# Forward transform over s of a spectral filter with three real products per complex one, and its edge column worked inside the last units

## The chip, the cores and the metric

The kernel runs on one core of a Trainium2 chip. The metric is the device time in microseconds (us) of one execution, and the time of a kernel is the median of several executions. A profile is one further execution, recorded by the hardware. The engines are called as in the profile: PE is TensorE (matmuls; PEld its weight loads), DVE is VectorE, ACT is ScalarE, POOL is GpSimd, SP is SyncE, which issues most DMAs.

## The reference

Two branches start from the layernorm of x, and their product is added to x:

```python
def _A_ref(x, w_r, w_i):
    B, S, D = x.shape
    X = jnp.fft.rfft2(x, axes=(-2, -1))
    X = X * (w_r + 1j * w_i)
    return jnp.fft.irfft2(X, (S, D), axes=(-2, -1))

def _B_ref(x, w1, w2):
    h = _silu(jnp.einsum("bsd,df->bsf", x, w1))
    return jnp.einsum("bsf,fd->bsd", h, w2)

x = A_x
xn = _layernorm(x, axis=-1)
s = _A_ref(xn, A_w_r, A_w_i)
g = _silu(_B_ref(xn, B_w1, B_w2))
return x + s * g
```

S is 2048, D is 1024, the hidden width is 3584, and everything is float32. The filter has 513 columns; the last, k = 512, is the edge column.

## The kernel before

**Products.** All matrix products run on fp16 halves: each factor is split into a high and a low part, and high·high, high·low and low·high are summed in PSUM. ACT makes a high part, DVE the low one. The first product (`pa`, L456) makes the hidden rows in 112 groups of 24 matmuls of 512 columns. The second (`pb`, L539 to L541) runs seven combined products m of halved operands, each in 8 groups j of 42 matmuls; a group is two *half products* of 21. Its weights come in tiles `jr`, are split by `w2_gen` into `w` and, for m = 4 and 5, are first summed by an accumulating DMA issued from POOL (`join`, L416). `acc` evacuates a group on DVE.

**Spectral filter.** `fd_gen` transforms along d, by 16 steps, and stores the halves of real and imaginary part in DRAM (`vd`). `f_gen` transforms along s in 16 *units* u (q = u//4, j = u%4). For a unit, `mat` (L947) issues 36 matmuls on the constants `kq` and the loaded `vq`: a step by 4 × 128 rows, each with a matmul of 256 columns that holds the real and imaginary part side by side (L954) and two of 128 that add the crossed terms (L955, L956). They fill one PSUM tile `fx` of 1024 columns; there are two buffers (tag `ft`). ACT copies half of the tile to `xc`, because the next additions need two inputs of which only one is read from PSUM: DVE's `xb` and `xd` (L1004, L1005), then a radix-4 step to `X`, the multiplication by the filter weights (`T`, L1019 and L1020), the sums `T` in place, `yb` and `yd` (L1036, L1037), and `Z` (L1055, most on DVE, a share on POOL). ACT's high part (L981) and DVE's low part (L986) of Z go to `zq`, a tile of four units with one buffer, which is stored to `zd` behind each fourth unit.

**Edge column.** `xsv` collects 24 values per row: the edge column of X, copied by POOL, and the filter's weights there. `edge_gen` is a job of its own behind `f_gen`: 12 small POOL copies (L1078 to L1081) into the tile `edge`, nine float32 matmuls with permutation matrices `perm` (`eps`, L1085 to L1087, a tile of tag `ft`), 31 POOL operations on 16 or fewer elements (L1095), a scaling and the halves `zp`, which a DMA turns over into `zps`.

**Inverse.** `i_gen` transforms back, along s (`iu`, L1204 and L1212) and along d (`id`, L1294). Its first job needs `zt` loaded from `zd`, and POOL's copy of `zps` into `zt` (L1173).

**What sets the order.** Each engine executes in the order in which this code issues. The outer loop issues one half product, and then `work` (L1447) issues one slot of the weight queue `wq` and up to three slots of the queue `bg` of spectral jobs. These are generators; a slot runs one to its next yield. A unit of `f_gen` has four slots, and its matmuls stand in the third. `work` ends when its own estimate of DVE's work (`clock`, filled by `meter` from `COST`) runs ahead of that of PE, so the number of slots per half product isn't fixed. `defer(n, ...)` issues something n half products later; `tile_of` and `store` do that for tiles of partial sums.

```python
COST = {"DVE": ("dve", 0.12, 1.05e-3), "PE": ("pe", 0.0, 0.4215e-3)}
...
clock["dve"] = max(clock["dve"], clock["pe"] - 1.0)
for _ in range(3):
    if clock["dve"] > clock["pe"] + LEAD or hold[0] or slot(bg) == PAUSE:
        break
```

Of the kernel before, what the change touches and what calls it, by code (L numbers as in the profile page):

```python
# [2 lines left out]

# [40 lines left out]
def make_constants():  # L44
# [16 lines left out]
    k = np.stack([-np.sin(th), np.cos(th), np.sin(th)], 3)  # L61
# [66 lines left out]
def spectral_ffn(ctx, tc, x, w_r, w_i, w1, w2, ca, kc, ci, tw, pm, out):  # L128
# [19 lines left out]
    vd = [dp.tile([128, 4, 4, 2, 256], F16, name=f"vd{j}") for j in range(4)]  # L148
    zd = [dp.tile([128, 4, 2, 1024], F16, name=f"zd{c}") for c in range(4)]
# [62 lines left out]
    COST = {"DVE": ("dve", 0.12, 1.05e-3), "PE": ("pe", 0.0, 0.4215e-3)}  # L212
# [190 lines left out]
    def w2_gen():  # L403
# [123 lines left out]
    def load_parts(m, j):  # L527
        for k in READS[m]:
            if (k, j) in part:
                continue  # L530
            t_ = tile_of(H["p"], [128, 512], F32, f"pl{m}_{j}_{k}", *home(m, j))
# [36 lines left out]
    def acc(m, j, ps, cols=slice(0, 512)):  # L568
# [7 lines left out]
        def keep(k, t_):  # L576
            store("pt", 3, lambda: nc.sync.dma_start(pd[k, j], t_))
# [217 lines left out]
    def fd_gen(c):  # L795
# [62 lines left out]
        o, sp = {}, {}  # L858

        def high_r(j):  # L860
            sp[j] = ap.tile([128, 4, 2, 256], F16, name=f"Rs{c}_{j}", tag="Rs", bufs=2)
            nc.scalar.activation(sp[j][:, :, 0], o[j], AF.Copy, scale=2.0**-21)

        def low_r(j):
            nc.vector.scalar_tensor_tensor(sp[j][:, :, 1], o[j], 2.0**-21, sp[j][:, :, 0], op0=OP.mult, op1=OP.subtract)
            defer(2, lambda: nc.sync.dma_start(vd[j][:, :, c], sp[j]))

        for j in range(4):
# [11 lines left out]
            o[j] = r.rearrange("a (q r) k -> a q (r k)", r=2)  # L880
            yield 3.9
# [36 lines left out]
    def open_f():  # L918
# [3 lines left out]
        B["k"], B["v"], B["w"], B["z"] = {}, {}, {}, {}  # L922

    def f_gen():
# [12 lines left out]

        def load_w(u):
# [8 lines left out]
        def mat(u):  # L947
            q = u // 4
            ps = pt.tile([128, 4, 2, 128], F32, name=f"fx{u}", tag="ft")
            v, k = B["v"].pop(u), B["k"][q]  # L950
            for c in range(4):
                o = ps[:, c].rearrange("m r k -> m (r k)")
                for n, (kh, vh) in enumerate(((0, 0), (0, 1), (1, 0))):
                    nc.tensor.matmul(o, k[:, c, kh, 1], v[:, c, vh], start=(n == 0), stop=False)  # L954
                    nc.tensor.matmul(ps[:, c, 0], k[:, c, kh, 2], v[:, c, vh, 128:256], start=False, stop=False)  # L955
# [669 lines left out]
```

## Time and profile before

| | us |
|---|---|
| median of 3 executions (lowest, highest) | 1237.54 (1236.69, 1238.83) |
| the profiled execution | 1235.84 |
| its span | 1234.1 |
| PE busy in it | 1220.7 |
| DVE busy | 999.0 |
| ACT busy | 467.6 |
| POOL busy | 117.3 |

The span runs from the first to the last recorded instruction; the rest of an execution's time lies around it. A row of a timeline gives the start and the duration of an instruction in us, then engine, line, operation, the tile written and the tiles read (`Z<-yb`), the shape of an operand (partitions x elements) and in brackets how long the engine had stood idle before, and what ended that. A row of a group gives busy us and mean ns of one. The parts of the kernel lie along the span as follows: first product to about 636 us, with `fd_gen` from 156 to 555; second product from there to the end; the units from 583 to 845; the inverse from 890.

### The profile page before, as it was taken

The page shows a single profiled execution, that of the slowest core. Times are in us where ns is not written, and L with a number is a line of the kernel's source. Part 1 is how long each engine was busy: PE and PEld are TensorE (multiplying, and loading weights), DVE is VectorE, ACT ScalarE, POOL GpSimd, SP SyncE. Part 2 cuts the span into 40 slices and gives each one's busy share as a digit, 9 for nine tenths or more (in the row PEclk, how much of TensorE's full clock was granted, in tenths as well). Part 3 has the DMA queues.
Part 4 walks back from the last instruction along what each step waited for, and adds up shares of the span by engine and source line. Part 5 has one row for each costly group of instructions (what it writes and reads, how often), then busy time and mean ns, then how long its engine had stood idle before and what let it go on. Part 6 is the DMA issues. An engine that isn't in the chain of part 4 may idle for free.

```text
span 1234.1 us, 19097 instructions
## 1 busy us (share of the span) xinstructions
PE 1220.7 (99%) x7033; PEld 625.2 (51%) x7033; DVE 999.0 (81%) x1970; ACT 467.6 (38%) x614; POOL 117.3 (10%) x245
## 2 busy tenths in 40 slices
PE   8999999999999999999999999999999999999998
PEld 5545445444544454445545555554455555555545
DVE  7687988899798898896969899985186678798886
ACT  4865344333554565444433222122032222243212
POOL 2330000001000000010001121114111111000000
PEclk9999999999999999999999999999999999999999
DMA  7487476655758898759898999997989999998576
GB/s 253 134 172 187 135 224 201 185 152 161 223 172 237 276 283 242 217 177 279 207 283 224 283 259 198 276 256 246 293 207 278 286 289 331 315 332 325 200 261 260
DMA packets 271102, 293.67 MB, mean 238 GB/s; under 512 B 40096, under 2 KB 198816, under 8 KB 270624
## 3 DMA queue, kind: packets, MB, share of 16 engines
q1 hardware_dynamic: 250992, 233.66, 65.7%
q10 hardware_dynamic: 15984, 51.45, 12.0%
q0 software_dynamic: 4032, 7.34, 3.5%
q8 instruction: 55, 0.90, 0.3%
q14 instruction: 39, 0.32, 0.1%
HBM read 185.95 MB, written 102.25 MB: 234 GB/s over the span
## 4 chain that ended last, share of the span: by engine, by line
PE 75%; DVE 11%; DMA 9%; issue 2%; ACT 1%; SPq 0%; POOL 0%; DVEq 0%; ACTq 0%; POOLq 0%
PE pa L456 45%; PE pb L539 8%; PE pb L541 8%; PE pb L540 8%; DVE Z L1055 2%; DMA wq<-in_A_w_i_dram 2%; DMA sd<-s 2%; PE id L1294 2%; DMA zd<-zq 1%; DMA ht<-hd_sum_d 1%; DVE T L1020 1%; DVE w L254 1%; PE iu L1204 1%; ACT xp L709 1%; PE iu L1212 1%
## 5 line engine op out<-in xcount | busy, mean ns | idle before, releaser
L456 PE MATMUL pa<-xnT,w 128*128 128x512 f16 x2688 | 585.2, 379 | 1.1 <-ACT w L251 0.7
L456 PEld LDWEIGHTS <-w 128*128 128x128 f16 x2688 | 262.2, 98 | 311.6 <-DVE w L254 1.3
L539 PE MATMUL pb<-w,ht 128*128 128x512 f16 (+2 forms) x812 | 300.4, 372 | 0.0
L540 PE MATMUL pb<-w,ht 128*128 128x512 f16 (+2 forms) x812 | 300.4, 372 | 0.0
L541 PE MATMUL pb<-w,ht 128*128 128x512 f16 (+2 forms) x812 | 300.3, 372 | 0.0
L541 PEld LDWEIGHTS <-ht 128*128 128x128 f16 x812 | 79.4, 98 | 91.0
L539 PEld LDWEIGHTS <-ht 128*128 128x128 f16 x812 | 79.5, 98 | 86.7
L540 PEld LDWEIGHTS <-ht 128*128 128x128 f16 x812 | 79.4, 98 | 86.7
L465 ACT ACTIVATE h<-pa,s 128x512 f32<-128x512 f32 x112 | 75.5, 678 | 122.9 <-PE pa L456 111.0
L251 ACT ACTIVATE w<-jr,sc 128x512 f16<-128x512 f32 x98 | 68.1, 713 | 77.8 <-PE pb L541 22.1
L254 DVE SCALAR_TENSOR_TENSOR w<-jr,sc,w 128x512 f16<-128x512 f32 x98 | 71.1, 744 | 2.1 <-ACT w L251 2.1
L254 DVE SCALAR_TENSOR_TENSOR hoone<-h,hs,hoone 128x2048 f16<-128x2048 f32 x28 | 65.6, 2344 | 7.9 <-ACT hoone L251 7.9
L251 ACT ACTIVATE hoone<-h,hs 128x2048 f16<-128x2048 f32 x28 | 56.0, 1998 | 36.5 <-DVE h L499 24.3
L251 ACT ACTIVATE hosum<-hr,hs 128x1536 f16<-128x1536 f32 x28 | 44.1, 1574 | 64.1 <-DVE hr L495 26.8
L981 ACT ACTIVATE zq<-Z,zs 128x1024 f16<-128x1024 f32 x16 | 18.4, 1149 | 103.9 <-DVE Z L1055 57.0
L494 DVE TENSOR_TENSOR hr<-h 128x1024 f32<-128x1024 f32 x28 | 34.2, 1221 | 24.4 <-ACT h L465 24.3
L254 DVE SCALAR_TENSOR_TENSOR hosum<-hr,hs,hosum 128x1536 f16<-128x1536 f32 x28 | 50.7, 1812 | 3.1 <-ACT hosum L251 3.1
L251 ACT ACTIVATE w<-w1r,rs 128x1024 f16<-128x1024 f32 x28 | 31.9, 1144 | 47.0 <-DVE w L254 31.8
L274 DVE TENSOR_REDUCE m<-w1r 128x1 f32<-128x1024 f32 x28 | 33.8, 1210 | 16.1 <-DMA w1r<-in_B_w_dram 16.1
L632 ACT ACTIVATE pl<-pl,c 128x512 f32<-128x512 f32 (+2 forms) x28 | 17.6, 657 | 70.1 <-DVE pl L608 41.6
L954 PE MATMUL fx<-vq,kq 128*128 128x256 f16 x192 | 43.2, 273 | 0.0
L955 PE MATMUL fx<-vq,kq 128*128 128x128 f16 x192 | 42.0, 219 | 0.0
(219 smaller groups left out, 1524.8 us busy)
## 6 DMA issues: line engine op xcount, KB each, us to landing
w1r<-in_B_w_dram SPq DMA_DIRECT2D x28, 512.0 KB, 6.2
hd_sum<-hosum SPq DMA_DIRECT2D x56, 256.0 KB, 2.9
hd_one<-hoone SPq DMA_DIRECT2D x56, 256.0 KB, 3.7
hd_dif<-hoone SPq DMA_DIRECT2D x56, 256.0 KB, 3.2
w2m<-in_B_w_dram SPq DMA_DIRECT2D x28, 512.0 KB, 5.2
ht<-hd_dif ACTq DMA_DIRECT2D x32, 448.0 KB, 6.3
jr<-in_B_w_dram SPq DMA_DIRECT2D x56, 256.0 KB, 6.8
ht<-hd_sum ACTq DMA_DIRECT2D x32, 448.0 KB, 6.4
```

What stands on the lines that cost most here:

```text
L251: nc.scalar.activation(hi, raw, AF.Copy, scale=scale)
L254: nc.vector.scalar_tensor_tensor(lo, raw, scale, hi, op0=OP.mult, op1=OP.subtract)
L274: nc.vector.tensor_reduce(m1[:, i:i + 1], raw[i], axis=AX.XY, op=OP.max, apply_absolute_value=True)
L456: nc.tensor.matmul(ps, w[:, wh, d], xt[:, xh, d], start=(n == 0), stop=(n == 23))
L465: nc.scalar.activation(hq[:, 2 * (c % 2) + f % 2], ps, AF.Silu, scale=s1[:, f:f + 1])
L494: tt(sums[:, 0:2], hq[:, 0::2], hq[:, 1::2], op=OP.subtract)
L539: nc.tensor.matmul(ps, hh[:, 0], w[:, 0], start=first, stop=False)
L540: nc.tensor.matmul(ps, hh[:, 0], w[:, 1], start=False, stop=False)
L541: nc.tensor.matmul(ps, hh[:, 1], w[:, 0], start=False, stop=last)
L954: nc.tensor.matmul(o, k[:, c, kh, 1], v[:, c, vh], start=(n == 0), stop=False)
L955: nc.tensor.matmul(ps[:, c, 0], k[:, c, kh, 2], v[:, c, vh, 128:256], start=False, stop=False)
L1055: eng.tensor_tensor(Z[:, ns, pos], x0[:, :, ls], x1[:, :, ls], op=o_)
```

## The change

**Three products.** With a constant c + i·s and data a + i·b, the changed `mat` makes c·(a+b), (s−c)·b and (−s−c)·a; the real and the imaginary part are the first plus the second and the first plus the third. The constants `kq` hold cos, sin − cos and −sin − cos in place of −sin, cos and sin. The sum a+b is the third operand: `fd_gen` makes it (`total`, one DVE addition a step), splits it (`both`, one ACT and one DVE instruction) and stores it (`vs`, 256 KB a step); `load_s` loads it two units ahead into `vs` tiles of its own tag with two buffers. A unit now has two PSUM tiles of 2 × 512 columns, of which 3 × 128 of each 512 are used, so it takes both buffers of `ft`. There are 36 matmuls of 128 columns.

**Sums.** ACT copies the shared product twice side by side into `xo` (two copies of 512 elements; `xo` shares tag `T1` with the products by the filter weights, `xc` is gone), DVE adds the two other products from PSUM in two additions of 512, and then `xb` and `xd` read SBUF.

**Edge column.** `edge_gen` is stepped inside units 12 to 15 instead of as a job behind them. Its tiles `edge` and `perm` come from the pool of partial sums, its PSUM tile from the pool of the products (tag `ff`), and the 16 small loads into `xsv` are issued in units 0 to 7 instead of 0 to 15.

**Room and order.** The weight tiles of the second product have 8 slots instead of 7; the eighth takes some partial sums for m = 4. The tiles `fs` and `fx` come from a pool opened after the filter's is closed. The fixed part of DVE's cost in `COST` is 0.09 until the inverse stage opens, and 0.12 from there.

```diff
-    k = np.stack([-np.sin(th), np.cos(th), np.sin(th)], 3)
+    k = np.stack([np.cos(th), np.sin(th) - np.cos(th), -np.sin(th) - np.cos(th)], 3)
...
-    COST = {"DVE": ("dve", 0.12, 1.05e-3), "PE": ("pe", 0.0, 0.4215e-3)}
+    COST = {"DVE": ("dve", 0.09, 1.05e-3), "PE": ("pe", 0.0, 0.4215e-3)}
...
-                w2t[m, q // 7] = fp.tile([128, 7, 2, 512], F16, name=f"w2_{m}_{q // 7}", tag="big", bufs=4)
+                w2t[m, q // 7] = fp.tile([128, 8, 2, 512], F16, name=f"w2_{m}_{q // 7}", tag="big", bufs=4)
...
         def high_r(j):
+            both[j] = ap.tile([128, 4, 2, 128], F16, name=f"vt{c}_{j}", tag="wd", bufs=3)
+            nc.scalar.activation(both[j][:, :, 0], total[j], AF.Copy, scale=2.0**-21)
...
+            nc.vector.scalar_tensor_tensor(both[j][:, :, 1], total[j], 2.0**-21, both[j][:, :, 0], op0=OP.mult, op1=OP.subtract)
+            defer(2, lambda: nc.sync.dma_start(vs[j][:, :, c], both[j]))
...
+            nc.vector.tensor_tensor(total[j], o[j][:, :, 0:128], o[j][:, :, 128:256], op=OP.add)
...
         def mat(u):
             q = u // 4
-            ps = pt.tile([128, 4, 2, 128], F32, name=f"fx{u}", tag="ft")
-            v, k = B["v"].pop(u), B["k"][q]
-            for c in range(4):
-                o = ps[:, c].rearrange("m r k -> m (r k)")
-                for n, (kh, vh) in enumerate(((0, 0), (0, 1), (1, 0))):
-                    nc.tensor.matmul(o, k[:, c, kh, 1], v[:, c, vh], start=(n == 0), stop=False)
-                    nc.tensor.matmul(ps[:, c, 0], k[:, c, kh, 2], v[:, c, vh, 128:256], start=False, stop=False)
-                    nc.tensor.matmul(ps[:, c, 1], k[:, c, kh, 0], v[:, c, vh, 0:128], start=False, stop=(n == 2))
-            psx[u] = ps
+            v, t_, k = B["v"].pop(u), B["s"].pop(u), B["k"][q]
+            for half in range(2):
+                ps = pt.tile([128, 2, 512], F32, name=f"fx{u}_{half}", tag="ft")
+                for i, c in enumerate((half, half + 2)):
+                    for g, src in enumerate((t_[:, c], v[:, c, :, 128:256], v[:, c, :, 0:128])):
+                        for n, (kh, vh) in enumerate(((0, 0), (0, 1), (1, 0))):
+                            nc.tensor.matmul(ps[:, i, 128 * g:128 * g + 128], k[:, c, kh, g], src[:, vh], start=(n == 0), stop=(n == 2))
+                psx[u, half] = ps
+            if u + 2 < 16:
+                defer(1, lambda: load_s(u + 2))
...
-            cps[u] = bp.tile([128, 2, 256], F32, name=f"xc{u}", tag="xc", bufs=1)
-            nc.scalar.activation(cps[u], psx[u].rearrange("m c r k -> m c (r k)")[:, 2:4], AF.Copy)
+            cps[u] = bp.tile([128, 2, 2, 2, 128], F32, name=f"xo{u}", tag="T1", bufs=1)
+            for half in range(2):
+                nc.scalar.activation(cps[u][:, half], psx[u, half][:, :, 0:128].unsqueeze(2).broadcast_to([128, 2, 2, 128]), AF.Copy)
...
+            full = cps.pop(u)
+            for half in range(2):
+                planes = psx.pop((u, half))[:, :, 128:384].rearrange("m i (r k) -> m i r k", r=2)
+                tt(full[:, half], full[:, half], planes, op=OP.add)
...
+            if u == 12:
+                B["edge"] = edge_gen()
+            if u > 13:
+                next(B["edge"])
             yield 2.8
...
+            if u == 12:
+                next(B["edge"])
+            if u > 13:
+                next(B["edge"])
             yield 2.3
...
+            if u > 13:
+                next(B["edge"])
             yield 2.5
...
+            if u > 12:
+                next(B["edge"], None)
             yield 2.9
...
-        ps = pt.tile([128, 1024], F32, name="eps", tag="ft")
+        ps = pf.tile([128, 512], F32, name="eps", tag="ff")
...
-                add(bg, edge_gen())
```

Where the instructions stand is seen in each engine's order. On PE the units' matmuls stood behind every 42 or 63 matmuls of the second product, and stand behind every 63. The edge matmuls stood 105 of them behind the last unit's; here is that place in the order before (a row is a line of the code, an operation and its tiles):

```order
L541 LDWEIGHTS ht_2_1_8059
L541 MATMUL pb_2_8256<-w_2_1_7449,ht_2_1_8059 128x512
L1085 MATMUL eps<-edge,perm 128x24
L1086 MATMUL eps<-edge,perm 128x8
L1087 MATMUL eps<-edge,perm 128x8
```

In the changed kernel they stand 21 behind the matmuls of unit 14, and 42 ahead of those of unit 15:

```order
L546 LDWEIGHTS ht_2_0_8081
L546 MATMUL pb_2_8362<-w_2_0_7167,ht_2_0_8081 128x512
L1123 MATMUL eps<-edge,perm 128x24
L1124 MATMUL eps<-edge,perm 128x8
L1125 MATMUL eps<-edge,perm 128x8
```

Counted from the last unit's matmuls they have moved from 105 behind to 42 ahead. POOL makes their input. Before, its 12 copies stood behind its share of the last unit's Z:

```order
L1055 TENSOR_TENSOR Z_8284<-yb_8248 128x2x16 x2
L1055 TENSOR_TENSOR Z_8284<-yd_8249 128x2x16 x2
L1078 COPY edge<-xsv 128x24
L1079 COPY edge<-xsv 128x8
L1080 COPY edge<-xsv 128x2
L1081 COPY edge<-xsv 128x6
```

In the changed kernel they stand behind unit 13's Z (Z_8333), and the first operations on the edge matmuls' result (L1133) ahead of unit 14's (Z_8533); from the last copies on:

```order
L1116 COPY edge<-xsv 128x24
L1117 COPY edge<-xsv 128x8
L1118 COPY edge<-xsv 128x2
L1119 COPY edge<-xsv 128x6
L1133 TENSOR_TENSOR edge<-xsv,edge 128x16 x3
L1133 TENSOR_TENSOR edge<-edge,xsv 128x16
L1133 TENSOR_TENSOR edge<-xsv,edge 128x16 x4
L1087 TENSOR_TENSOR Z_8533<-yb_8518 128x2x16 x2
L1087 TENSOR_TENSOR Z_8533<-yd_8519 128x2x16 x2
```

So the edge column's POOL work went from behind the units to between the Z of the last three. Further on POOL's queue, the first inverse job's copy of the edge column (`zt<-zps`) stood behind three of the accumulating weight DMAs that follow the edge column's work, and stands behind seven (the last six of them shown):

```order
L418 DMA jr_8704<-in_B_w_dram 128x512
L418 DMA jr_8749<-in_B_w_dram 128x512
L418 DMA jr_8785<-in_B_w_dram 128x512
L418 DMA jr_8876<-in_B_w_dram 128x512
L418 DMA jr_8908<-in_B_w_dram 128x512
L418 DMA jr_8934<-in_B_w_dram 128x512
L1213 COPY zt_8817<-zps 128x16
```

The copy has moved with the inverse stage, which begins 84 matmuls of the second product later, while the weight DMAs keep their places beside the second product.

More of the change, by code (lines that the diff above doesn't have):

```diff
@@ L2 @@
 from contextlib import ExitStack
+from types import SimpleNamespace
 import numpy as np
@@ L148, in spectral_ffn @@
     vd = [dp.tile([128, 4, 4, 2, 256], F16, name=f"vd{j}") for j in range(4)]
+    vs = [dp.tile([128, 4, 4, 2, 128], F16, name=f"vs{j}") for j in range(4)]
     zd = [dp.tile([128, 4, 2, 1024], F16, name=f"zd{c}") for c in range(4)]
@@ L576, in keep @@
         def keep(k, t_):
-            store("pt", 3, lambda: nc.sync.dma_start(pd[k, j], t_))
+            store("big" if m == 4 and j % 2 else "pt", 3, lambda: nc.sync.dma_start(pd[k, j], t_))
         def evac():
@@ L1063, in edge_gen @@
     def edge_gen():
-        bp = B["p"]
         g = nc.gpsimd
         xv = xsv
-        perm = B["perm"]
-        room, used = bp.tile([128, 1024], F32, name="edge", tag="T1", bufs=1), [0]
+        room, perm = (tile_of(H["p"], [128, 512], F32, name, "pt", 6) for name in ("edge", "perm"))
+        perm = perm[:, 0:384].rearrange("m (n k) -> m n k", n=3)
+        nc.sync.dma_start(perm, pm[:, 0:3])
+        used = [0]
+        yield
         def piece(n):
+            if used[0] + n > 512:
+                used[0] = 0
             used[0] += n
@@ L1150, in open_i @@
         C["ci"] = C["p"].tile([128, 2, 4, 2, 256], F16, name="cis")
+        COST["DVE"] = ("dve", 0.12, 1.05e-3)
         C["z"], C["k"] = {}, {}
```

36 lines of the change are left out of this document (23 added, 13 removed).

## The prediction

> **What bounds it.** I read the page's busy shares and its chain first, then the waits of PE, then the stage that the change rewrites.
>
> ```profile
> span 1234.1 us, 19097 instructions
> PE 1220.7 (99%) x7033; PEld 625.2 (51%) x7033; DVE 999.0 (81%) x1970; ACT 467.6 (38%) x614; POOL 117.3 (10%) x245
> PE 75%; DVE 11%; DMA 9%; issue 2%; ACT 1%; SPq 0%; POOL 0%; DVEq 0%; ACTq 0%; POOLq 0%
> PE tp L718 <- ACT x L709: 3.0, 3, 2.0
> PE iu L1212 <- DVE ub L1221: 1.7, 1, 1.7
> ```
>
> PE (TensorE) is busy 99% of the span. The last two rows are from the view of waits (engine and line, what it waited for; us in total, times, longest): the largest belongs to the start-up (L718 transposes x), the next is one wait in the inverse transform. So between the first matmuls and the last PE goes from one matmul to the next without a pause: the end is the sum of PE's work, and any microsecond taken from PE's instruction stream is gained, unless some engine then can't keep up and PE waits. Windows through the forward stage show who could fail (us; busy us and count of PE, weight loads, DVE, ACT, POOL; clock, DMA share, GB/s):
>
> ```profile
> 652.70:845.00 192.30, 192.15 (x1184) 103.74 (x1181) 177.60 (x328) 46.37 (x66) 32.87 (x70) 1.00 0.93 246
> 684.90:701.00 16.10, 16.10 (x100) 8.61 (x99) 10.33 (x19) 4.05 (x6) 0.47 (x2) 1.00 0.99 329
> 701.00:717.00 16.00, 16.00 (x100) 8.59 (x98) 15.90 (x32) 2.23 (x3) 3.73 (x8) 1.00 0.97 223
> 156.00:560.00 404.00, 404.00 (x2101) 193.68 (x2100) 346.83 (x681) 188.19 (x224) 19.61 (x34) 1.00 0.71 212
> ```
>
> The granted clock is 1.00. DVE (VectorE) is busy without a gap in 701–717 and idle in 684.9–701; it swings between late and stalled, while PE never notices. The slack between DVE and PE is what the change spends.
>
> **The matmuls (the gain).** One unit's matmuls and their neighbour (start us, duration us; a duration includes the pipeline, so I use differences of starts):
>
> ```profile
> 650.12 0.27 PE L954 MATMUL fx<-vq,kq 128*128 128x256 f16 x1
> 650.23 0.22 PE L955 MATMUL fx<-vq,kq 128*128 128x128 f16 x1
> 650.28 0.22 PE L956 MATMUL fx<-vq,kq 128*128 128x128 f16 x1
> ...
> 652.77 0.38 PE L539 MATMUL pb<-w,ht 128*128 128x512 f16 x1
> 895.68 2.68 PE iu L1204 x48
> 100.83 5.18 PE pa L456 x24
> L954 PEld LDWEIGHTS <-kq 128*128 128x128 f16 x192 | 18.8, 98 | 1.9
> L1204 PEld LDWEIGHTS <-zt 128*128 128x128 f16 x192 | 11.2, 98 | 1.4
> ```
>
> A unit is 36 matmuls, 12 of 256 columns and 24 of 128, in 2.65 us. After it is 36 of 128 columns, each with weights of its own. The chain of waits has the same form: 48 matmuls L1204 of 128 columns, each behind a weight load, in 2.68 us, 55.8 ns each. So 36 × 0.0558 = 2.01 us, 0.64 less, and 16 × 0.64 = **10.2 us** less. It is the same as the difference of columns: 1536 columns a unit at 5.18/24/512 = 0.42 ns. No matmul of the two products changes in number. The Trainium skill speaks against this gain ("TensorE: Matmul & The Clock Gate", § Back-to-back issue gap): it gives a stream of weight load and matmul pairs about 81 ns a matmul at 128 columns, by which, as an estimate, a unit would cost 36 × 81 = 2.92 us and the stage 4.3 us more than before. The rows of this case, 55.8 ns in such a stream, disagree.
>
> **Additions ahead of the stage.** The third operand costs 16 DVE additions, 16 low parts and 16 ACT high parts, each of 512 elements, and 16 writes of 256 KB.
>
> ```profile
> 717.54 0.68 DVE L1004 TENSOR_TENSOR xb<-fx,xc 128x512 f32<-128x512 f32 x1
> 718.14 0.68 DVE L1005 TENSOR_TENSOR xd<-fx,xc 128x512 f32<-128x512 f32 x1
> L254 DVE SCALAR_TENSOR_TENSOR w<-jr,sc,w 128x512 f16<-128x512 f32 x98 | 71.1, 744 | 2.1 <-ACT w L251 2.1
> ```
>
> By xb, 0.60 us from start to start, and a weight tile's low part of 512, 0.74, that is 16 × 1.34 = 21 us of DVE in the 156–560 window, where it has 57 us free, and DMA runs at 0.71. Cost on PE: nothing; without that cover it would be late by what is missing.
>
> **DVE inside the units.** Each unit gets two more additions of 512 elements that read PSUM, as xb does, and loses nothing: +1.20 us.
>
> ```profile
> 696.98 1.28 DVE L986 SCALAR_TENSOR_TENSOR zq<-Z,zs,zq 128x1024 f16<-128x1024 f32 x1 [5.36 <-ACT zq L981]
> 808.10 1.28 DVE L986 SCALAR_TENSOR_TENSOR zq<-Z,zs,zq 128x1024 f16<-128x1024 f32 x1 [7.98 <-ACT zq L981]
> zd<-zq SPq DMA_DIRECT2D x16, 512.0 KB, 7.2
> ```
>
> The 192.3 us window holds 13 units: 177.60/13 = 13.66 us of DVE each, 14.86 after. Units now come irregularly, after 42 or 63 matmuls of the second product; in the new order always after 63, so every 63 × 0.2158 + 2.01 = 15.6 us. DVE has 0.7 us to spare per unit, if its stalls go. These are the two in the rows: every fourth unit ACT's high part needs the one zq buffer, which the four stores to zd free (median landing 7.2 us), and DVE's low part waits for ACT. Between the stores and that high part lies less than a unit; at 15.6 us the unit gives up to 3.9 us more than the short ones of 11.7 (42 matmuls), so I count on much shorter stalls. If both stay, 13.3/13 = 1.0 us a unit is more than the spare, and DVE falls behind by some 0.3 us a unit. ACT's two copies of 512 elements a unit take the place of one; ACT is busy 46 of 192 us, so nothing. The 16 loads of 256 KB add 17 GB/s to 246, where other windows reach 329: nothing, as long as they are asked for two units ahead.
>
> Both PSUM buffers now belong to one unit, so the next unit's matmuls wait for these additions. They come 13.6 us after the unit's matmuls end. Before, the corresponding readers ended late at worst here:
>
> ```profile
> 804.24 0.22 PE L956 MATMUL fx<-vq,kq 128*128 128x128 f16 x1
> 813.63 0.68 DVE L1037 TENSOR_TENSOR yd<-T 128x512 f32<-128x512 f32 x1
> 818.05 0.68 DVE L1005 TENSOR_TENSOR xd<-fx,xc 128x512 f32<-128x512 f32 x1
> 720.35 0.22 PE L956 MATMUL fx<-vq,kq 128*128 128x128 f16 x1
> 725.59 0.68 DVE L1037 TENSOR_TENSOR yd<-T 128x512 f32<-128x512 f32 x1
> ```
>
> Unit 14's xd ended 818.73, 14.4 us behind matmuls that ended 804.30, with the 7.98 stall in it; without, 6.5. So this new wait costs between 0 and 0.8 us once; I take 0, nearer to the unit without stall.
>
> **The edge column moved inside the units.** Before, its matmuls stood 105 second-product matmuls behind the last unit's; now only 21 behind unit 14's, and their input is copied by POOL (GpSimd) behind unit 13's Z, which needs unit 13's yd. So PE gets a new wait, and behind it stand all matmuls of the kernel. The pieces, from unit 15 of before:
>
> ```profile
> 840.39 0.68 DVE L1037 TENSOR_TENSOR yd<-T 128x512 f32<-128x512 f32 x1
> 845.03 0.18 POOL L1081 COPY edge<-xsv 128x6 f32<-128x6 f32 x1
> 843.20 0.30 PE L1085 MATMUL eps<-edge,perm 128*128 128x24 f32 x2
> 845.00 0.38 PE L1085 MATMUL eps<-edge,perm 128*128 128x24 f32 x2
> 845.66 0.38 PE L539 MATMUL pb<-w,ht 128*128 128x512 f16 x1
> ```
>
> From yd's end (841.07) to the end of the last copy (845.21) are 4.14 us. On PE, the last three edge matmuls start 21 × 0.2158 + 1.80 = 6.33 us behind unit 14's, the 1.80 being the first six. With x for how long after unit 14's matmuls unit 13's yd ends, PE waits x + 4.14 − 6.33 = x − 2.2. Before, x was 814.31 − 804.30 = 10.0 there (and 726.27 − 720.41 = 5.9 for unit 7). The interval in question becomes 15.6 instead of 42 × 0.2158 + 2.65 = 11.7, which takes 3.9, and the additions give 1.2: x = 7.3 if the stall recurs. Without the stall and nothing else changed, 10.0 − 7.98 = 2.0. I take the middle, 4.6: **+2.4 us**, with 0 and 5.1 as ends.
>
> POOL's edge work now runs beside DVE's last three units:
>
> ```profile
> 590.11 0.68 DVE L1055 TENSOR_TENSOR Z<-yb 128x128 f32<-128x128 f32 x2
> 814.23 0.91 DVE L1055 TENSOR_TENSOR Z<-yb 128x128 f32<-128x128 f32 x2
> 813.85 1.03 POOL L1055 TENSOR_TENSOR Z<-yb 128x32 f32<-128x32 f32 x2 [18.74 <-DVE yb L1036]
> ```
>
> The same DVE addition takes 0.68 us alone and 0.91 beside POOL; a third more on DVE's work in the 4.14 us above is at most 1.4 us, inside the range of x. The Trainium skill says that GpSimd shares its SBUF interfaces with VectorE ("GPSIMD Engine Reference", § 1. Specifications), contending where an instruction has two SBUF inputs; these rows agree.
>
> **The inverse stage and the tail.** The first inverse unit needs POOL's small copy of the edge column, which stands behind weight joins on POOL's queue, three before and seven after:
>
> ```profile
> 890.43 0.85 POOL L1173 COPY zt<-zps 128x16 f16<-128x16 f16 x1
> L416 POOL DMA_DIRECT2D jr<-in_B_w_dram x7: 853/868/1191, 869.4 to 899.3; - x7
> DMA to landing us min/median/max: 4.4/7.8/14.9
> ```
>
> The copy ended 891.28 and L1204 started 895.68: 4.4 us of slack. The last join's load is recorded two half products, 9.1 us, ahead of the copy; at the median landing of 7.8 it costs nothing, at 14.9 it costs 14.9 − 9.1 − 4.4 = 1.4, and with three joins of 0.87 left to issue 4.0. I take **+0.5**, near the median. Larger weight tiles, a slot for partial sums in them, and the pool opened late only move storage; the last inverse matmuls end 252 second-product matmuls (54 us) before PE's end, so nothing.
>
> **Sum.** −10.2 + 2.4 + 0.5 = −7.3. The profiled execution took 1235.84 us (1234.1 and 1.7 around it), so 1228.5 by its clock; it lies 1.7 under the median of 1237.54. From the median: **1230.2 us**.
>
> **Rivals.** A: *no new wait.* DVE, evenly loaded, finishes yd within 2.2 us of the next matmuls. For it: regular intervals; against: x was 5.9 in an undisturbed unit. −10.2: 1227.3.
>
> B: *DVE becomes the bound at the end of the stage.* Stalls on zq stay, 0.3 us a unit add up over 13 units to 3.9, and x reaches 8.5 to 10. The wait at the edge matmuls is 6.3 to 7.8, with the 0.5: 1234 to 1235.6. For it: only 0.7 us spare, DMA at 0.93 of its time. Against: the stores get a longer unit to land in.
>
> C: *the joins hold the edge copy.* +4.0 in place of 0.5: 1233.7. For it: POOL waits for its loads' landing; against: the median of 7.8.
>
> D: *weight loads set the pace, and the change is slower.* If a matmul of 128 columns can't start faster than its weight load lasts, a unit is 36 × 0.098 = 3.53 us, 0.88 more: +14.1, 1251.6. It decides as soon as the spacing is over 2.65/36 = 73.6 ns. Against: L1204's loads also last 98 ns, and run at 55.8, so they overlap. The Trainium skill's 81 ns ("TensorE: Matmul & The Clock Gate", § Back-to-back issue gap) lies on this side: by it, as an estimate, +4.3 and the two waits, 1244.7.
>
> **Chances.** Forecast 0.50 (1228.4 to 1233), A 0.20, B 0.15, C 0.11, D 0.04. A measurement of this kernel tells about 0.2%, 2.5 us, from no change: faster is below 1235.1. The forecast, A, C and half of B lie there, 0.89; the rest of B is within, 0.07; D is slower, 0.04. The range 1226.5 to 1235.5 leaves out D, a little of A and the end of B.
>
> **What would show it.** Right: a unit of matmuls of 2.0 us; a wait of PE at the edge matmuls of 1 to 5 us on POOL's copies, and no wait at fx. A is shown by no such wait, B by one over 6 us or waits at fx on DVE's additions, and zq stalls in DVE's rows; C by a wait of iu on the copy of zt; D by a unit over 2.65 us. What would make it wrong altogether is a wait that I have put at nothing: the third operand's load landing late, or DVE late ahead of the stage.

## The result, and the profile after

| | before | changed |
|---|---|---|
| median of 5 executions, us (lowest, highest) | 1236.69 (1235.1, 1238.83) | 1266.55 (1264.93, 1269.16) |
| profiled execution, us | 1235.84 | 1264.93 |

The changed kernel is slower: the ratio is 1.024, interval 1.0225 to 1.0255, some 30 us, where 7 less were forecast. The page of the changed kernel has these answers to the rows shown of before:

```profile
span 1263.2 us, 19218 instructions
PE 1223.6 (97%) x7033; PEld 622.8 (49%) x7033; DVE 1039.6 (82%) x2034; ACT 482.2 (38%) x646; POOL 124.9 (10%) x245
PE 44%; DVE 27%; DMA 19%; issue 4%; SPq 3%; ACT 3%; ACTq 0%; POOL 0%; DVEq 0%; POOLq 0%
```

The chain of waits is no longer PE's: its share fell from 75% to 44%, and DVE and DMA have most of what it lost. The view of PE's waits (what it waited for; us, times, longest) says where:

```profile
PE id L1334 <- DVE sk L1348: 6.8, 1, 6.8
PE pa L458 <- ACT h L467: 6.2, 2, 3.2
PE eps L1123 <- POOL edge L1116: 5.9, 1, 5.9
PE pb L544 <- DMA ht<-hd_dif: 4.3, 2, 2.4
PE iu L1252 <- DVE ub L1261: 3.6, 2, 3.1
...
PE fa L787 <- ACT L L797: 1.5, 1, 1.5
```

Here `iu` and `id` are the inverse's matmuls along s and along d, `ub` and `sk` DVE's steps on their results, `h` the hidden rows as ACT evacuates them, and `fa` matmuls of `fd_gen`. All but 1.7 us (iu) of these waits are new. They don't account for everything, because PE's busy time rose too, although it has less to do. Windows around the wait for the edge column (busy us of PE, weight loads, DVE, ACT, POOL; then the granted clock) show why:

```profile
836.00:842.00 6.00, 6.00 (x56) 3.85 (x55) 2.23 (x4) 2.37 (x3) 0.00 (x0) 1.00 1.01 248
842.00:849.00 7.00, 1.17 (x6) 0.32 (x4) 6.96 (x12) 1.08 (x2) 2.11 (x6) 0.91 0.99 311
849.00:852.00 3.00, 2.90 (x14) 2.90 (x14) 3.00 (x8) 2.30 (x3) 2.40 (x12) 0.50 1.09 74
852.00:855.00 3.00, 3.00 (x11) 1.68 (x11) 2.90 (x7) 1.04 (x3) 1.52 (x5) 0.50 0.92 189
855.00:858.00 3.00, 3.00 (x9) 1.07 (x8) 3.00 (x4) 0.01 (x1) 3.00 (x5) 0.51 1.03 402
858.00:861.00 3.00, 3.00 (x15) 1.36 (x14) 2.35 (x4) 0.00 (x0) 0.40 (x1) 1.00 0.80 310
...
780.00:783.00 3.00, 1.12 (x7) 0.33 (x5) 3.00 (x9) 0.67 (x2) 0.89 (x3) 1.00 1.04 404
783.00:786.00 3.00, 3.00 (x16) 1.35 (x15) 2.90 (x6) 1.32 (x2) 0.00 (x0) 1.00 0.99 352
```

Behind the stop of 6 us PE's granted clock is 0.50 for 9 us, and its matmuls take twice as long (0.43 us from start to start instead of 0.22); behind the stop of 2 us at 780 it stays 1.00.

**Where the time went, by stage.** Both kernels issue the same 2688 + 2436 matmuls of the two products in the same order. I took the start of one and the same such matmul in both traces, where all work of a stage lies ahead of it in both: the 2416th of the first product (ahead of the first unit), the 881st of the second (all units and the edge column done), the last. The differences to before grow by **+12.0 us ahead of the units, +4.3 with the units and +12.8 in the inverse and the tail**, 29.1 in all. Without the gain of 10.2 the units are 14.5 worse.

### The profile page after: what moved, and what is told of

Its sections match the earlier page's. It is cut to its first block, busy times and chain, and to the rows that moved or that the text cites. A ratio compares the mean times of both kernels' runs of the same rounds, so it can differ in the third digit from the quotient of the medians.

```text
span 1263.2 us, 19218 instructions
## 1 busy us (share of the span) xinstructions
PE 1223.6 (97%) x7033; PEld 622.8 (49%) x7033; DVE 1039.6 (82%) x2034; ACT 482.2 (38%) x646; POOL 124.9 (10%) x245
## 4 chain that ended last, share of the span: by engine, by line
PE 44%; DVE 27%; DMA 19%; issue 4%; SPq 3%; ACT 3%; ACTq 0%; POOL 0%; DVEq 0%; POOLq 0%
PE pa L458 21%; PE pb L545 6%; PE pb L544 6%; PE pb L546 6%; DMA jr<-in_B_w_dram 3%; DVE w L256 2%; DMA sd<-s 2%; DVE Z L1087 2%; DMA ws<-wd 2%; DVE hoone L256 2%; DMA vs<-vt 2%; SPq L490 1%; DVE wd L377 1%; DVE hosum L256 1%; DMA ht<-hd_sum_d 1%
## 5 line engine op out<-in xcount | busy, mean ns | idle before, releaser
L256 DVE SCALAR_TENSOR_TENSOR hoone<-h,hs,hoone 128x2048 f16<-128x2048 f32 x28 | 65.7, 2345 | 11.6 <-ACT hoone L253 11.6
L995 ACT ACTIVATE xo<-fx 128x512 f32<-128x512 f32 x32 | 17.5, 594 | 73.0 <-DVE yd L1067 48.5
L276 DVE TENSOR_REDUCE m<-w1r 128x1 f32<-128x1024 f32 x28 | 33.8, 1211 | 13.2 <-DMA w1r<-in_B_w_dram 13.2
L1087 POOL TENSOR_TENSOR Z<-yb 128x32 f32<-128x32 f32 x32 | 16.1, 522 | 216.5 <-DVE yb L1066 216.5
L418 POOL DMA_DIRECT2D jr<-in_B_w_dram x28 | 24.8, 1010 | 126.0 <-DMA jr<-in_B_w_dram 47.0
```

Source lines behind the costliest of these rows:

```text
L256: nc.vector.scalar_tensor_tensor(lo, raw, scale, hi, op0=OP.mult, op1=OP.subtract)
L276: nc.vector.tensor_reduce(m1[:, i:i + 1], raw[i], axis=AX.XY, op=OP.max, apply_absolute_value=True)
L418: nc.gpsimd.dma_start(raw[n], w2_block(*todo[n], 1), accum_op=OP.add)
L995: nc.scalar.activation(cps[u][:, half], psx[u, half][:, :, 0:128].unsqueeze(2).broadcast_to([128, 2, 2, 128]), AF.Copy)
L1087: eng.tensor_tensor(Z[:, ns, pos], x0[:, :, ls], x1[:, :, ls], op=o_)
```

## The experiments

The kernel before had medians of 1236.6 to 1238.3 beside these. The last four columns are differences to before in the profiled executions, by the stages above. Each row of them is one execution: before_late and late_rows issue up to the inverse what the kernel before issues, and still have +3.2 and +1.1 in the units, most of it at the edge column's matmuls. So a term of 3 us alone says little. Kernels that leave out work (no_sum, pe_clean, b1_nosum, b1_noadds, late_rows, after_rows, pe_only) don't compute the reference; they only locate time.

| kernel | median us | ahead of units | units | inverse | sum |
|---|---|---|---|---|---|
| changed | 1266.55 | +12.0 | +4.3 | +12.8 | +29.1 |
| no_sum | 1251.47 | +1.0 | +2.2 | +14.0 | +17.2 |
| edge_later | 1266.87 | +13.9 | −7.5 | +23.6 | +30.0 |
| ht_sp | 1269.92 | +12.0 | +4.6 | +14.8 | +31.5 |
| before_late | 1255.23 | +0.2 | +3.2 | +16.6 | +20.0 |
| edge_dve | 1265.11 | +13.8 | −6.0 | +21.9 | +29.6 |
| lag0 | 1265.07 | +12.5 | +4.5 | +8.6 | +25.6 |
| fd_fix | 1263.45 | +5.9 | +7.9 | +14.1 | +27.8 |
| best1 | 1260.23 | +14.7 | −4.2 | +15.9 | +26.4 |
| pe_clean | 1242.11 | −0.1 | −10.7 | +13.8 | +2.9 |
| b1_nosum | 1251.78 | +2.4 | −3.8 | +14.8 | +13.3 |
| b1_noadds | 1254.03 | +1.7 | +7.1 | +10.3 | +19.1 |
| before_adds0 | 1244.41 | +0.0 | +3.0 | +4.0 | +7.0 |
| late_rows | 1247.46 | −0.2 | +1.1 | +10.8 | +11.6 |
| after_rows | 1262.47 | +12.4 | +2.0 | +10.5 | +24.8 |
| pe_only | 1245.01 | +0.3 | +0.1 | +8.3 | +8.8 |
| pl_pt | 1270.27 | +14.5 | +5.4 | +16.0 | +35.9 |
| fd_own2 | 1280.34 | +19.6 | +13.7 | +13.2 | +46.5 |
| best5 | 1279.85 | +18.9 | −0.3 | +24.1 | +42.8 |

### The third operand (no_sum, fd_fix, fd_own2)

```diff
-            total[j] = ap.tile([128, 4, 128], F32, name=f"vt{c}_{j}", tag="E", bufs=1)
-            nc.vector.tensor_tensor(total[j], o[j][:, :, 0:128], o[j][:, :, 128:256], op=OP.add)
...
-            nc.sync.dma_start(B["s"][u], vs[j][:, q])
+            nc.sync.dma_start(B["s"][u], vd[j][:, q, :, :, 0:128])
```

> The changed kernel without the third operand's making: fd_gen's additions, its halves and its store to vs are left out, and the units load the real part from vd in its place, as many bytes. Theory (in the stage ahead of the units ACT waits for buffers that the third operand shares with the weight sums, and for its last store, and PE then waits for ACT three times, 1.5, 3.3 and 3.1 us, with the granted clock at 0.5 behind the two long ones): these three waits go, 12 us with the clock, 1254.5. Rival (the stage is late because the units' first slots are recorded earlier, not because of these buffers): the waits stay, 1265 to 1267.

All three waits ahead of the units (fa 1.5, pa 3.2 and 3.0) are gone, 11 us with the clock, and the median is 15 lower. So the third operand's making costs it. How, is seen in ACT's timeline of the changed kernel (in brackets, how long it had stood idle and what ended that):

```profile
532.70 0.63 ACT L867 ACTIVATE vt<-vt 128x512 f16<-128x512 f32 x1 [2.82 <-DMA ws<-wd]
...
570.68 0.39 ACTq L940 DMA_DIRECT2D kq<-in_kc_dram  x1
571.12 0.69 ACT L467 ACTIVATE h<-pa,s 128x512 f32<-128x512 f32 x1 [14.95 <-DMA vs<-vt]
```

The operand's high part waits for a buffer of the ring `wd`, which it shares with the weight sums, until one of their stores lands. Later ACT's load of `kq` waits 15 us for the last store of the operand, since the units' pool takes its place. Behind both stands ACT's evacuation `h<-pa`, for which PE waits. fd_fix stores it one half product sooner and gives that load to SP:

```diff
-            defer(2, lambda: nc.sync.dma_start(vs[j][:, :, c], both[j]))
+            defer(1, lambda: nc.sync.dma_start(vs[j][:, :, c], both[j]))
...
-            nc.scalar.dma_start(t_, kf[q])
+            (nc.sync if q == 0 else nc.scalar).dma_start(t_, kf[q])
```

> The changed kernel with the store of the third operand issued one half product sooner, and the first load of kq issued by SP instead of ACT. Theory (ACT's queue stands still, first for shared buffers whose stores are late, then behind the load of kq that waits for the last store): the wait at 568 goes with its half clock, 4.5 us, and half of the one at 531, 3 us: 1258 to 1262. Rival (SP's queue, which carries the hidden rows' stores, stands still in ACT's place): no gain, 1265 to 1270.

Ahead of the units 6.1 of the 12.0 went, where 7.5 were expected, and not as expected: the wait at 568 is gone, and so is the one at fa, but the one at 531 grew from 3.2 to 4.2 us, with ACT's wait for the ring at 4.0. The units lost 3.6: PE now waits 3.2 us at fx, half of it for the operand's loads, which stand behind on SP. fd_own2 was to settle the ring:

```diff
-            both[j] = ap.tile([128, 4, 2, 128], F16, name=f"vt{c}_{j}", tag="wd", bufs=3)
+            both[j] = ap.tile([128, 4, 2, 128], F16, name=f"vt{c}_{j}", tag="vt", bufs=2)
...
-                nc.scalar.activation(junk, t_, AF.Abs, accum_out=w2m[:, i - 3:i - 2])
+                nc.scalar.activation(t_, t_, AF.Abs, accum_out=w2m[:, i - 3:i - 2])
```

> The changed kernel with the third operand's halves in a ring of two buffers of their own (the weight sums keep two, and the room is that of the scratch tile of the weights' maximum, which is now taken in place), and the first load of kq issued by SP. Theory (ACT stands still for the shared ring and behind the load of kq, and nothing else of the third operand costs time): the 12 us ahead of the units shrink to 0 to 3, 1255 to 1258. Rival (the work itself, ACT's and DVE's additions to the stage, makes PE wait): 6 us or more stay there, 1260 or more.

A miss by its own doing. The room came from taking the maximum in place, and ACT's waits show what that costs:

```profile
ACT w2m L383 <- DVE wd L376: 98.1, 17, 13.3
```

ACT may overwrite the tile only when DVE has read it, and stood still for 98 us. That the ring alone makes the first wait is therefore seen in the trace, not shown by a run. best5 is this with edge_dve and lag0. At 1279.85 it missed its forecast of 1239 to 1249 by the same cause, and says no more; no kernel here beats the one before.

> fd_own2 with the edge column later, its copy on DVE and the inverse opened two pauses sooner (first inverse matmuls at 1071), a kernel that computes all. Theory (terms add: ahead of the units 0 to 3, units -7, inverse 8 to 16): 1239 to 1249, so no gain against before. Rival (with all of its waits' causes gone it keeps most of its 10.2): 1233 or less.

### The edge column (edge_later, edge_dve)

```diff
-            if u > 13:
+            if u > 14:
                 next(B["edge"])
             yield 2.8
```

> The changed kernel with the edge column's matmuls recorded two slots later, behind unit 15's matmuls instead of 21 behind unit 14's, and the rest of the edge work as much later. Theory (PE's 6.1 us wait there is for POOL's copies behind a late unit 13, and the half clock behind it costs 3.9 more): 10 us less, 1256.5. Rival (DVE is late as a whole, and the next thing that PE needs of it waits instead, unit 15's matmuls for unit 14's additions, or the first inverse unit): 3 us less or nothing, 1263.5 to 1266.5.

The theory came true for the wait and the rival for the time. The units are 11.8 us better (from +4.3 to −7.5), some 10 of it the wait with its half clock. And the median is the same, since the inverse took 10.8 of it, and the stage ahead of the units the rest:

```profile
PE iu L1246 <- POOL zt L1215: 8.8, 1, 8.8
```

This is the joins that hold the edge copy, rival C, which the earlier stop had covered. edge_dve issues that copy on DVE:

```diff
-            nc.gpsimd.tensor_copy(zt[:, :, :, :, 0, 0], zps[:, :, c])
+            (nc.vector if c == IORDER[0] else nc.gpsimd).tensor_copy(zt[:, :, :, :, 0, 0], zps[:, :, c])
```

> The kernel edge_later with the first inverse job's copy of the edge column into zt issued on DVE instead of POOL. Theory (with the wait at the edge matmuls gone, PE reaches the first inverse matmuls sooner and there waits 8.8 us for this copy, which stands on POOL's queue behind seven weight joins): the wait goes with the half clock behind it, 12 us less than edge_later, 1255. Rival (zt or zps itself lands late, whoever copies): the wait stays, now behind DVE's copy, 1265 to 1268, or more where DVE is held by it.

Its theory held for the wait and not for the time. The first inverse matmuls now start without a wait, 34.1 us behind DVE's last low part of the units instead of 43.0 (48.3 in the kernel before), but at a later inverse unit PE waits 7.0 us for DVE's `ub`, and the inverse's term fell by 1.7 only.

### The loads of ht (ht_sp)

In the units of the changed kernel ACT waits 25.5 us for stores of zq, and 47 us for yd, the last reader of the products whose buffer `xo` now shares. The loads of ht stand behind on its queue. Below these two rows is the first of the stops, which ends with the landing of a load that ACT issued at 771.58, behind a high part for which it had waited 9.4 us:

```profile
ACT xo L995 <- DVE yd L1067: 47.2, 9, 8.4
ACT zq L1001 <- DMA zd<-zq: 25.5, 3, 9.4
...
771.56 1.15 ACT L1001 ACTIVATE zq<-Z,zs 128x1024 f16<-128x1024 f32 x1 [9.40 <-DMA zd<-zq]
782.53 0.39 PE L544 MATMUL pb<-w,ht 128*128 128x512 f16 x1 [1.88 <-DMA ht<-hd_dif]
```

```diff
-                    load_h(*seq[n + 2], k, nc.scalar)
+                    load_h(*seq[n + 2], k, nc.sync)
```

> The changed kernel with the second product's loads of ht issued from SP's queue instead of ACT's. Theory (the two waits for ht at 780 and 798 us, 2.0 and 2.6, come because the loads stand on ACT's queue behind instructions that wait for the zq store and for yd): both go, 4.6 less, 1262. Rival 1 (the loads are late by their transfer, with DMA at 1.0 of its time): no change, 1266.5. Rival 2 (SP's queue waits longer than ACT's): slower, above 1270.

Both waits went, but two others came, 5.7 us at 718 and 1.6 at 917, so the waits for ht grew from 4.3 to 7.3 us; the units' term is as before, and the median lies between the two rivals'. SP's queue is no freer. That the first stop comes from ACT's wait is read in the trace, not shown by a run; the load behind the second took 16.35 us from issue to landing, so the transfer has a part in that one. Nothing here shows how to get the loads past.

### The place of the inverse (before_late, lag0, late_rows, after_rows, pl_pt)

```diff
-                add(bg, switch(B, open_i, 6, lag=2))
+                add(bg, switch(B, open_i, 6, lag=6))
```

> The kernel before with nothing changed but four more pauses ahead of the inverse stage, so that every inverse matmul stands behind as many matmuls of the second product as in the changed kernel (the first 84 later). Theory (the inverse stage's waits in the changed kernel, 6.8 for id and 3.2 for iu, 12.8 us with the clock against before, come from this place alone, where its DVE work and loads meet those of m = 4): about 12 us slower than before, 1248 to 1250. Rival (they come from DVE's lag out of the units, the eighth slot of the weight tiles or the later pool): within 2 us of before, 1236 to 1239.

The clearest run of all: the kernel before, with only the inverse recorded 84 matmuls later, loses 16.6 us in it; the whole takes 1.0141 (1.0125 to 1.0156) times as long as before. That is more than the 12 expected. PE's and DVE's waits of before_late:

```profile
PE iu L1212 <- DVE ub L1221: 9.6, 1, 9.6
PE id L1294 <- ACT w L251: 4.1, 1, 4.1
...
DVE pl L623 <- DMA fs<-sd: 18.8, 3, 9.0
```

DVE finishes row blocks of m = 4 with filter rows `fs`, loaded from DRAM. In the kernel before it never waits for them in this stretch; here, as in the changed kernel (12.7 us), the rows have only just been made when they are due, so the load is asked for right ahead of its use, and what stands behind on DVE, the inverse's `ub`, is late for PE. late_rows reads x in their place:

```diff
-        for name, src, (tag, bufs) in (("fs", sd[c, p], tags[0]), ("fx", xs[4 * c + p], tags[1])):
+        for name, src, (tag, bufs) in (("fs", xs[4 * c + p], tags[0]), ("fx", xs[4 * c + p], tags[1])):
```

> The kernel before_late, where the last step for a row block reads x a second time in place of the filter's row from DRAM (so the filter's part of these rows is left out), with as many bytes. Theory (in before_late DVE waits 18.8 us for rows that the inverse stored just before they are reloaded, and PE for DVE): these waits go, 10 to 14 us less than before_late, 1241 to 1245. Rival (the weights' joins and DVE's load in this place make it): 1253 or more.

8 us less, not 10 to 14. The store's way goes, but DVE waits all the same:

```profile
DVE pl L623 <- DMA fs<-in_A_x_dram: 15.2, 3, 8.2
```

The load behind the longest of these waits is issued at 1050.42, 2.0 us after DVE began to wait for it, and lands at 1056.50. So it is the late asking more than the store. after_rows is the same edit in the changed kernel:

> The changed kernel, where the last step for a row block reads x a second time in place of the filter's row from DRAM (the filter's part of these rows is left out). Theory (the inverse's waits in the changed kernel are the reload's too, 12.7 us on DVE): the wait of iu goes and part of the one of id, 6 to 10 us less, 1256 to 1261. Rival (the one of id, 6.8, is the weight loads', and the gain is taken by another): 1263 or more.

It gave 1262.47: the wait of id shrank to under 1 us, and iu's grew from 3.6 to 8.9, the other way round from its theory; as its rival has it, another wait took the gain. lag0 opens the inverse two pauses sooner:

```diff
-                add(bg, switch(B, open_i, 6, lag=2))
+                add(bg, switch(B, open_i, 6, lag=0))
```

> The changed kernel with the inverse stage opened two pauses sooner, so that its first matmuls stand 42 matmuls of the second product earlier (1071 instead of 1113; 1029 in the kernel before), and its third job on at the places of before. Theory (the inverse's place is what makes DVE wait 12.7 us for rows that were stored just before, and PE for DVE): the waits at id and at the second job's iu go, 10 to 13 us less, 1254 to 1257. Rival 1 (DVE's lag out of the units makes them): they stay, 1264 to 1268. Rival 2 (zt, loaded 9 us sooner, lands late and PE waits at the first iu instead): 1258 to 1264.

The median, 1265.07, is what rival 1 forecast. In the profiled execution, the fastest of four with 1261.43, the inverse's term fell from 12.8 to 8.6 and id's wait from 6.8 to 1.1, while iu first waited 1.9 for the edge copy: by its waits in between the theory and rival 2. pl_pt puts the partial sums of m = 4 back into their pool:

```diff
-            if m == 4 and k == 0 and j % 2:
-                t_ = w2t[m, j // 2 % 2][:, 7].rearrange("p h x -> p (h x)").bitcast(F32)
```

> The changed kernel with the partial sums of m = 4 in the pool they had before instead of the weight tiles' eighth slot. Theory (the slot has no part in the inverse's waits): 1264 to 1269. Rival (weight tiles wait for partial sums stored from their slot, and id and iu behind them): 1258 or less.

1270.27: the eighth slot isn't the cause, and taking it away gains nothing.

### The gain alone, and the work it brings (best1, pe_clean, b1_nosum, b1_noadds, before_adds0, pe_only)

best1 is edge_dve, lag0 and fd_fix together with DVE's cost at 0.07. b1_nosum leaves out the third operand's making (as no_sum), b1_noadds DVE's additions in the units, and pe_clean both, with every inverse matmul at one place:

```diff
-                tt(full[:, half], full[:, half], planes, op=OP.add)
```

> All of these together (edge column later, its copy on DVE, inverse opened two pauses sooner, the third operand's store sooner, kq by SP) with DVE's fixed cost at 0.07, which puts every inverse matmul but the first job's first at the place of before. Theory (each wait has its own place and cause): what is left is the 10.2 us of gain against the two ht waits (4.6) and half of the wait at 531 (3 to 5): 1233 to 1238. Rival (the work that the change adds to DVE has to be waited for somewhere): waits of 6 us or more come up elsewhere, 1245 or more.

best1 took 1260.23, as its rival said: PE waits 5.3 and 3.0 us ahead of the units, 3.2 at fx and 6.9 at iu.

> The matmuls of the change without the work that they bring to DVE: the third operand isn't made (fd_gen's additions, halves and store are left out, the units load the real part instead) and DVE's two additions from PSUM in each unit are left out; the edge column later, its copy on DVE and the inverse opened two pauses sooner, as in best1, so that every inverse matmul stands where it stands in best1. Theory (the gain on PE is there, and DVE's added work eats it): no wait over 2 us is left, 10 us less than before, 1226 to 1231. Rival (both PSUM buffers in one unit and the matmuls' form bring waits of their own): 1237 or more.

The gain is there: −0.1 and **−10.7** up to the end of the units, with no stop of PE over 0.6 us between 50 us and 889. Then the inverse takes 13.8, and the median, 1242.11, lies in the rival's range, though not by the rival's cause. DVE's copy of the edge column stood 11.59 us for zt, and PE behind it:

```profile
893.27 0.21 DVE L1208 COPY zt<-zps 128x16 f16<-128x16 f16 x1 [11.59 <-DMA zt<-zd]
```

The last of the four loads of zt landed at 893.05, and the constants `kk` for the same matmuls at 894.13, 0.04 us ahead of PE's start: all of the first job's loads are late, not the copy alone. Here the first inverse matmuls stand 252 matmuls behind the last unit's; in the kernel before it was 336, in the changed one 294, since its last unit moved back by 126 and the inverse only by 84. So opening the inverse sooner, as in lag0, takes from the time in which zq is stored and zt loaded. No run has the new matmuls with 336.

before_adds0 gives the kernel before the additions alone:

```diff
-            tt(b.rearrange("m c r k -> m c (r k)"), pv[:, 0:2], cpy, op=OP.add)
+            for _ in range(3):
+                tt(b.rearrange("m c r k -> m c (r k)"), pv[:, 0:2], cpy, op=OP.add)
```

> The kernel before, with its own matmuls, where DVE makes xb three times over, that is two more additions of 512 from PSUM in each unit; DVE's fixed cost at 0.09 up to the inverse and the inverse opened two pauses sooner, so that every inverse matmul stands where it stands in best1. Theory (DVE has no room for 19 us more in this stretch): PE waits for DVE at fx or iu, 6 to 12 us and its half clock: 1244 to 1252. Rival (DVE has room; only the changed kernel's buffers make it late): 1236 to 1240.

The median lies at the low end of the theory's range, but by luck: PE waits only 1.3 us for DVE, at iu, not 6 to 12, so my theory that DVE has no room fell here. Two more additions a unit cost PE 0.8 us up to the last unit. The rest of the 7.0 comes at the edge column (+2.2, no more than before_late shows there without any addition) and in the inverse (+4.0), where PE waits 2.8 us for POOL's edge copy.

> best1 without the third operand's making (left out in fd_gen, the units load the real part instead), with DVE's additions in the units. Theory (the waits ahead of 640 us are those of the third operand's making, some 11 us and their half clock): 14 to 17 us less than best1, 1243 to 1246. Rival (removing one wait only lets another grow): 1252 or more.

> best1 with the third operand made, without DVE's two additions in each unit (left out), DVE's fixed cost at 0.09. Theory (the waits behind 700 us, at fx 3.2 and at iu 6.9, 1.9 and 1.3, come from DVE being late by these additions): 12 to 16 us less than best1, 1244 to 1248. Rival (they come from the place of the edge column and the inverse): within 5 us of best1, 1255 or more.

They gave 1251.78 and 1254.03, both slower than their theories and close to their rivals: against pe_clean the additions cost 9.7, the third operand 11.9 and both 18.1, by the medians. In b1_noadds PE waits 3.5 us for the operand's loads and 4.2 for the weights' split. pe_only is pe_clean with edge column and opening as in the change:

> The changed kernel without the third operand's making and without DVE's two additions (both left out as in pe_clean), with the edge column, its copy and the opening of the inverse as in the change; the first inverse matmuls stand at 1092. Theory (PE keeps its 10.2 us up to the inverse, whose place costs about as much): no wait over 2 us ahead of 880 us, 10 us less there, and 8 to 14 more in the inverse: 1235 to 1242. Rival (the inverse costs only where DVE and ACT have the change's added work): 1227 to 1232.

```profile
PE eps L1116 <- POOL edge L1109: 6.4, 1, 6.4
```

Even with neither addition nor operand PE waits 6.4 us at the edge matmuls; its units' term is 10.8 worse than pe_clean's. That wait comes with the edge column's place, even without DVE's added work. The inverse costs 8.3. The forecast of no wait over 2 us ahead of it was wrong at this one place.

## Why the prediction was wrong

**The matmuls (−10.2): right.** Unit 5 of the changed kernel starts at 691.38 and the next product matmul at 693.39:

```profile
691.38 0.33 PE L971 MATMUL fx<-vs,kq 128*128 128x128 f16 x3
...
693.39 0.38 PE L544 MATMUL pb<-w,ht 128*128 128x512 f16 x1
```

2.01 us, 55.8 ns a matmul; the gain shows undiluted in pe_clean. Rival D is out, and the 81 ns of the Trainium skill ("TensorE: Matmul & The Clock Gate", § Back-to-back issue gap) with it: the trace doesn't agree.

**"Cost on PE: nothing" ahead of the stage: wrong, 12.0.** The step counted DVE's free 57 us and never asked for which buffers and behind whom the new instructions wait. ACT was the engine, with less than half of its time used: not its load but its order, a shared ring and a pool whose opening waits for the last store. no_sum shows that the operand's making costs this, fd_fix that the pool has a part; the ring's part is read in the trace alone. The prediction named as its dangers the operand's load landing late and DVE late ahead of the stage; it was neither.

**The edge column (+2.4): right mechanism, wrong size, 9.9.** The formula x − 2.2 held: unit 14's matmuls ended at 838.47 and unit 13's yd (row below) at 847.34, so x was 8.9 instead of 4.6, beyond the 7.3 that I had as its upper end, and 6.7 stands against a measured 5.9. The stall whose end I counted on came back, at 3.8 us instead of 8.0 (row below), right ahead of this yd. By the prediction's own sum that gives an x of 3.1, so 5.8 more come from DVE being behind, though it worked without a pause from 808 to the stall; why stays open. The additions alone aren't the reason: in pe_only, which has none, x is 9.3. This is rival B's x of 8.5 to 10 with its stall, without its waits at fx. The rest, 4 us, is the half clock (8.8 us of work at 0.50), which the prediction had for no wait. pe_only and edge_later show that the place costs this much.

```profile
840.60 1.28 DVE L1006 SCALAR_TENSOR_TENSOR zq<-Z,zs,zq 128x1024 f16<-128x1024 f32 x1 [3.77 <-ACT zq L1001]
846.66 0.68 DVE L1067 TENSOR_TENSOR yd<-T 128x512 f32<-128x512 f32 x1
849.10 0.62 PE L1123 MATMUL eps<-edge,perm 128*128 128x24 f32 x2 [5.94 <-POOL edge L1116]
```

**DVE and ACT inside the units (0): wrong, 4.6 (the two stops for ht).** I expected shorter stalls for zq and set ACT's copies to nothing by its busy time. DVE's stalls did get shorter, from 14.6 to 7.6 us in all, but ACT's waits for zq stores rose from 9.8 to 25.5 us, and ht loads behind them were late. That this is the whole cause is argued, not shown (ht_sp moved the loads and gained nothing). The wait at fx that I weighed didn't come.

**The inverse (+0.5): wrong, 12.8.** I priced only the edge copy. The step "the last inverse matmuls end 252 second-product matmuls (54 us) before PE's end, so nothing" looked at the end of a chain whose middle is due earlier: m = 4 needs the first inverse job's rows. before_late shows the place alone can cost this and more. Of the 12.8, the share of the rows, of the weights' joins and of the copy stays open: each run that took one away let another grow.

29.1 = −10.2 + 12.0 + 9.9 + 4.6 + 12.8. Of the 39.3 lost (29.1 and the 10.2 of gain), 26.4 are new stops of PE (its idle time between 100 and 1210 us, 28.3 instead of 1.9), and 12.6 are half clock: 25.2 us of PE's work lie at 0.50 there, and half of that is lost; together 39.0.

**Could it have been read from before?** Its rows showed PE hardly ever waiting, and DVE in the units swinging between late and stalled. They did not show how near the other chains were; before_late does: 84 matmuls, 18 us, of slack less for the rows of m = 4, and 16.6 are lost.

## What to carry to other kernels

When one engine never waits in a kernel whose order is written by hand, the other chains may all have been placed to be just in time, as here; a saving on that engine brings each of its later steps forward against them. Price a moved or added instruction by what it waits for and what stands behind it on its queue, engine idle or not, and look at each consumer's due time, not at the stage's end. Add to each PE wait of over 3 us the half clock behind it.

## What the runs showed of the hardware

In the 20 traces I took each stop of PE of 1.2 us or more between 100 and 1210 us (from start to start, less the 0.22 us of a matmul), and the granted clock in the five us behind it. All 53 stops of 3.2 us or more had the clock at half for part of that time; of 20 between 2.5 and 3.2 us 12 had; of 52 shorter ones 8, but of these 8 five have another stop of 1.0 us 1.3 us behind them, and one has a stop of 5.3 us. In the changed kernel the half clock costs 12.6 of 1263 us. The Trainium skill ("TensorE: Matmul & The Clock Gate", § What's actually happening) says that the clock is halved after at least one idle window of about 3.4 us, which runs freely. The traces agree for the stops longer than that; that stops of 2.5 to 3.2 us can have it too is more than this section says.
